# Rows of q, X and the output ordered by parity, and the filter turned by parity, in a gated mix of an FFT convolution and an MLP

## The chip, the cores and the metric

The kernel runs on one core of a Trainium2 chip. Its engines each work through their own queue in order: TensorE (PE in the profile; PEld is its weight loads), VectorE (DVE), ScalarE (ACT), GpSimd (POOL) and the sync engine (SP), which here issues DMAs. Matmuls write to PSUM; VectorE and ScalarE bring the results back to SBUF. The metric is the device time of one execution in microseconds (us). Before the change it is 241.14 us, the median of three runs (241.05 to 241.84).

## The reference

Three things are computed from `x = q` (2048 rows of 640) and mixed by a gate per row.

```python
g = sigmoid((q * gate_w).sum(-1, keepdims=True))
# A: a long convolution along the rows, one filter per column
kv = k_shift * v                       # k_shift: 4 taps of k along the rows
y  = irfft(rfft(pad(kv)) * rfft(pad(ssm_k)))[:2048] + kv * ssm_D
a  = q * y
# B: a mixer and an MLP
h  = gelu(layernorm(q) @ w1)           # its four column groups are then shifted
x1 = q + shifted(h) @ w2               # by 1, -1, 2, -2 rows
b  = x1 + gelu(layernorm(x1) @ w3) @ w4
out = g * a + (1 - g) * b
```

Inputs and output are bf16.

## The kernel before

**Layout.** The 2048 rows are 128 groups of 16. A group lies on one partition (`q_rows`, `o_rows`, `v_rows`, `k_rows`: partition p holds rows 16p to 16p + 15), and the 16 places in a group are called t1. X, the output and the q tiles have group p on partition p. V, and k by way of its transposes, are ordered by parity instead: partitions 0 to 63 hold the even groups and 64 to 127 the odd ones (`HALF`). V gets that order from an indirect DMA that GpSimd issues with a list of row numbers (`take`, `v_load`, `row_order`).

**The convolution** is a Fourier transform of 4096 points in steps. `tap` makes kv: four taps of the turned k by matmuls on four 32-row array tiles, and products with V. `step1` transforms over the partitions, for kv (`KV`) and for the filter (`HT0`). For kv the two parities are two matmuls, each with 64 contraction rows, on the upper and the lower half of the array (line 424); for the filter they are two matmuls with all 128 rows, against a table `F1N` made for the plain order (line 422). The filter comes in with channels on partitions and is turned by 16 transposes of 128x128 for each of five column blocks (`h_transpose`, line 395). Results go to DRAM scratch (`S_x`, `S_h`) and come back in another order (`gather`); `step2` transforms over the 16 places; `product` multiplies; `step3` goes back, by way of scratch `S_g` and `gin`; `step4` is the last inverse step: two matmuls of 128x320 that add up in one PSUM bank, against two tables in `F4` with zeros in every second column (line 882), then times the gate and q, and added to the MLP's result in X.

**The MLP.** `x_stats`, `x_norm` and `x_turn` normalise and turn four chunks of four places; `mlp1` multiplies by w1; `h_shift` builds the shifted rows, with `turn` for those that pass to the neighbour group (one copy by one partition-row of columns); `w2`, `x1_norm`, `w3`, `w4` follow. `store` writes two places (or one) at a time.

**Order.** Everything is issued in an order written out by hand as a list of steps (`ORDER`), a name, its arguments, the engine for each eviction (A or V) and a part. Each engine takes its instructions in that order. PSUM has 4 banks for the convolution (`psc`) and 2 pairs for the MLP (`psm`). The places in the shared SBUF rings are written out as well (`SLOTS`); the ring "row" has four places, for k, normalised chunks, step 1 and step 3 results, q tiles and the last gin tile. DMAs from hardware queues share eight completion semaphores in turn, so that an issue also waits for the landing of the eighth issue before it.

The lines that matter below: 422 and 424 (step 1), 395 (transposes of the filter), 369 and 371 (evictions on ScalarE and VectorE), 587, 596, 599, 602 (taps: matmuls, copies, products), 707 (mlp1), 784 (w2), 832 (w3), 854 (w4), 882 to 896 (step 4), 174 (indirect DMA), 190 and 193 (X loads), 215 (w4 load), 534 (gin), 846 (stores), 865 (q loads).

Of the kernel before, what the change touches and what calls it, by code (L numbers as in the profile page):

```python
# [16 lines left out]
P = 128  # L17
# [4 lines left out]
H = 64  # L22
# [19 lines left out]
def kernel(  # L42
# [24 lines left out]
        "c": "012312031203132103210322130123013021203123012032112300312012013021302101320130213102301230132103"  # L67
             "120132013023102302101301231201032013210312031203021321002312032012332013210132032101203103212033"
             "021320121031302210321301302310212032031210323101032210323103201302131022310132031202130213021302"
             "130310231032301230120",  # L70
        "m": "0101011010101010101010101010101010101010101010101010101010100101010",
        "row": "01230120312013312013021032103213201202020",
        "gt": "012301212210202103201301201",
        "xt": "010101",
        "gq": "01221011201201201210201210201201201",
        "ax": "0123230123102301",
        "hp": "01231203",
# [31 lines left out]
    F1N = const.tile([P, 2, H, 2], BF16, name="F1N")  # L109
    F4 = const.tile([P, 2, H, 2], BF16, name="F4")  # L110
# [65 lines left out]
    def flat(x):  # L176
        return x.rearrange("p t d -> p (t d)")
# [10 lines left out]

    def load_x(c):
        SP.dma_start(out=flat(X[:, 4 * c:4 * c + 4, :]), in_=q_rows[:, 4 * c * D:4 * c * D + 4 * D])  # L190

    def load_x0(h):
        SP.dma_start(out=flat(X[:, 2 * h:2 * h + 2, :]), in_=q_rows[:, 2 * h * D:2 * h * D + 2 * D])
# [92 lines left out]
    def f1n_table():  # L286

        ts(col(27), bit(0), -1.0, pf[:], op1=ALU.add)
        ts(col(28), col(27), 0.5)
        n = tab([P, H, 2], "n")  # L290
        ts(n[:, :, 0], R64[:, 0:H], col(27), col(28))
        ts(n[:, :, 1], n[:, :, 0], float(128 + 128), op0=ALU.add)
        ts(n[:, :, 0], n[:, :, 0], float(64 + 128), op0=ALU.add)
        yield from sin_table(F1N[:, 0], n, 256)
        yield
        V.tensor_scalar(out=F1N[:, 1], in0=F1N[:, 0], scalar1=bit(0), scalar2=None, op0=ALU.mult)
        V.tensor_tensor(out=F1N[:, 0], in0=F1N[:, 0], in1=F1N[:, 1], op=ALU.subtract)

    def f4_table():
# [11 lines left out]
        V.memset(F4[:], 0.0)  # L311
        yield from sin_table(F4[:, 0, :, 0], n, 256)
        A.activation(out=F4[:, 1, :, 1], in_=n[:], func=ACT.Sin, scale=TWO_PI / 256 * SH, bias=NPI[:])
# [70 lines left out]
    def h_transpose(dc, ev):  # L384
        if "HT0" not in st:
            st["HT0"] = main.tile([P, NT * D], BF16, name="HT0", tag="RT")
        hv = st.pop(("HN", dc)).rearrange("p (q t1) -> p t1 q", t1=NT)
        dst = st["HT0"][:].rearrange("p (t d) -> p t d", t=NT)
        def make(hh):
            box = {}  # L390

            def first():
                ps = box["ps"] = slot(psc, [P, 8, P], BF16, "pst", "c", 4)
                for i in range(8):
                    PE.transpose(out=ps[:, i, :], in_=hv[:, 8 * hh + i, :], identity=IDB[:])  # L395

            def second():
                evac(ev[hh], dst[:, 8 * hh:8 * hh + 8, dc * P:(dc + 1) * P], box["ps"][:])
            return first, second

        return banks(2, make)
# [7 lines left out]
    def step1(name, c, ev):  # L409
# [5 lines left out]
        def make(u):  # L415
            ps = []

            def first():
                for r in range(2):
                    ps.append(slot(psc, [P, 512], F32, "ps1", "c", 4))  # L420
                    if name == "HT0":
                        PE.matmul(ps[r][:], lhsT=F1N[:, r].rearrange("p a b -> p (a b)"), rhs=src[:, o + 512 * u:o + 512 * u + 512], start=True, stop=True)  # L422
                    else:
# [686 lines left out]
```

## Time and profile before

| | |
|---|---|
| median of three runs | 241.14 us |
| profiled execution: its time, its span | 242.25 us, 240.5 us |
| TensorE busy, share of the span | 223.2 us, 93% |
| VectorE busy | 188.6 us, 78% |
| ScalarE busy | 178.4 us, 74% |
| GpSimd busy | 16.4 us, 7% |
| granted TensorE clock, mean | 0.993 |
| DMA: moved, mean rate | 57.10 MB, 237 GB/s |
| matmuls of filter step 1 (L422) | 40, mean 379 ns |
| matmuls of kv step 1 (L424) | 40, mean 382 ns |
| transposes of the filter (L395) | 80, mean 226 to 228 ns |
| matmuls of step 4 (L882) | 64, mean 299 ns |

The profile is of one execution, in microseconds from the start of its span. An instruction's duration includes the passage through the pipeline, so that matmuls overlap and a mean of 380 ns stands beside a start every 216 ns; times of whole blocks in the chain of waits are the better price. The chain follows the work that ended last back from its end. A table of waits gives, for an engine and line, what it waited for, the total, the times, and the longest. Stretches give busy time of each engine, the granted clock and the DMA share.

### The profile page before, as it was taken

The numbers are of one execution on the slowest core, as the hardware profiler recorded it, in microseconds if no ns is written. First come the engines' busy times: TensorE is split into PE (matmuls) and PEld (weight loads), VectorE is DVE, ScalarE is ACT, GpSimd is POOL, SyncE is SP. The second block draws the span as 40 slices with busy tenths as digits, with TensorE's granted clock in tenths as the row PEclk, the third lists the DMA queues.
The fourth block names the chain that finished last, engine by engine and source line by source line (L and its number), as shares of the span: only waits on it lengthen the run. The fifth ranks groups of instructions, "written<-read, shape, count | busy, mean of one in ns | idle before, by whom it ended". The sixth has DMA issues, their size and how long they took to land.

```text
span 240.5 us, 5957 instructions
## 1 busy us (share of the span) xinstructions
PE 223.2 (93%) x2401; PEld 113.3 (47%) x2420; DVE 188.6 (78%) x448; ACT 178.4 (74%) x320; POOL 16.4 (7%) x34
## 2 busy tenths in 40 slices
PE   8669679999999999999799999999999999999993
PEld 3455345433656555444345344444444455447551
DVE  6899587989999999974658896395995997308994
ACT  4599957989978998899977698769777543447480
POOL 3172202000000020022200000000000000000000
PEclk9999979999999999999999999999999999999999
DMA  6999975460599799999795928099755113889664
GB/s 222 371 376 408 369 168 139 92 237 1 221 326 417 222 328 285 269 415 344 226 294 142 178 96 277 4 343 311 168 188 220 59 54 118 267 303 375 225 252 187
DMA packets 42889, 57.10 MB, mean 237 GB/s; under 512 B 20329, under 2 KB 35690, under 8 KB 42606
## 3 DMA queue, kind: packets, MB, share of 16 engines
q1 hardware_dynamic: 42286, 54.10, 68.8%
q0 software_dynamic: 576, 2.62, 2.7%
q8 instruction: 19, 0.31, 0.5%
q14 instruction: 8, 0.07, 0.1%
HBM read 34.42 MB, written 18.36 MB: 219 GB/s over the span
## 4 chain that ended last, share of the span: by engine, by line
PE 74%; DMA 17%; DVE 4%; SPq 2%; issue 1%; POOL 1%; ACT 0%; DVEq 0%
PE ps L854 19%; PE ps L832 19%; PE psw L784 9%; PE psm L707 7%; DMA W<-in_B_w_dram 5%; DMA KV<-in_A_v_dram,ROWS 5%; PE ps L462 4%; DMA X<-in_A_q_dram 4%; PE ps L422 4%; PE ps L509 3%; DMA gin<-S_g 3%; PE ps L424 3%; PE pst L395 2%; PE psk L587 2%; PE ps L882 2%; DVE b L682 1%
## 5 line engine op out<-in xcount | busy, mean ns | idle before, releaser
L854 PE MATMUL ps<-W,gt 128*128 128x128 bf16 (+1 forms) x370 | 55.0, 296 | 2.5 <-DMA W<-in_B_w_dram 1.2
L832 PE MATMUL ps<-x1t,W 128*128 128x512 bf16 x240 | 55.2, 380 | 0.2 <-ACT gt L837 0.2
L854 PEld LDWEIGHTS <-gt 128*128 128x128 bf16 x384 | 29.0, 98 | 26.6 <-issue 4.8
L832 PEld LDWEIGHTS <-W 128*128 128x128 bf16 x240 | 22.2, 98 | 28.2 <-issue 4.2
L837 ACT ACTIVATE gt<-ps 128x1024 bf16<-128x1024 f32 x24 | 24.8, 1034 | 7.6 <-PE ps L832 7.6
L369 ACT CAST stg<-ps 128x512 bf16<-128x512 f32 x47 | 25.5, 598 | 6.2 <-PE ps L424 4.0
L369 ACT CAST gs<-ps 128x320 bf16<-128x320 f32 x42 | 15.6, 434 | 16.2 <-PE ps L509 10.4
L707 PE MATMUL psm<-xt,WA 128*128 128x512 bf16 x100 | 25.0, 396 | 0.5 <-DVE xn L661 0.5
L371 DVE CAST stg<-ps 128x512 bf16<-128x512 f32 x33 | 21.9, 686 | 1.8 <-PE ps L424 0.8
L784 PE MATMUL psw<-WA,HT 128*128 128x512 bf16 (+1 forms) x111 | 20.8, 296 | 0.2
L369 ACT CAST hs<-ps 128x512 bf16<-128x512 f32 x28 | 15.0, 597 | 5.9 <-PE ps L462 5.9
L886 ACT ACTIVATE y<-ps,GS 128x320 bf16<-128x320 f32 x25 | 11.9, 526 | 7.2 <-PE ps L882 4.7
L371 DVE CAST gs<-ps 128x320 bf16<-128x320 f32 x22 | 10.1, 485 | 7.9 <-PE ps L509 6.5
L371 DVE CAST XS<-ps 128x512 bf16<-128x512 f32 x15 | 10.0, 686 | 7.4 <-PE ps L462 7.1
L707 PEld LDWEIGHTS <-WA 128*128 128x128 bf16 x100 | 9.3, 101 | 12.7 <-issue 3.5
L369 ACT CAST XS<-ps 128x512 bf16<-128x512 f32 x25 | 13.5, 595 | 2.1 <-PE ps L462 2.1
L784 PEld LDWEIGHTS <-HT 128*128 128x128 bf16 x116 | 10.0, 98 | 10.5 <-PE ps L424 0.7
L861 DVE SCALAR_TENSOR_TENSOR X<-ps,OMG,X 128x640 bf16<-128x640 f32 x15 | 13.2, 877 | 0.4 <-PE ps L854 0.3
L462 PE MATMUL ps<-ax,CMP 64*32 64x384 bf16 (+3 forms) x512 | 13.1, 300 | 0.0
L786 DVE SCALAR_TENSOR_TENSOR X<-psw,X 128x640 bf16<-128x640 f32 x16 | 12.9, 816 | 0.1
L789 ACT ACTIVATE jk<-X 128x640 bf16<-128x640 bf16 x16 | 12.3, 767 | 0.0
L487 DVE TENSOR_TENSOR XS<-XS,hs 128x2560 bf16<-128x2560 bf16 x8 | 11.9, 1485 | 0.1
(151 smaller groups left out, 342.8 us busy)
## 6 DMA issues: line engine op xcount, KB each, us to landing
S_x<-stg SPq DMA_DIRECT2D x8, 640.0 KB, 4.0
S_h<-stg SPq DMA_DIRECT2D x8, 640.0 KB, 8.6
ax<-S_x SPq DMA_DIRECT2D x8, 640.0 KB, 6.0
ax<-S_h SPq DMA_DIRECT2D x8, 640.0 KB, 5.6
S_g<-gs SPq DMA_DIRECT2D x8, 640.0 KB, 4.8
W<-in_B_w_dram SPq DMA_DIRECT2D x2, 1920.0 KB, 10.6
kn<-in_A_k_dram SPq DMA_DIRECT2D x4, 640.0 KB, 11.0
q<-in_A_q_dram SPq DMA_DIRECT2D x4, 640.0 KB, 5.0
```

The lines of the kernel that those rows point to most:

```text
L369: A.copy(out=dst, in_=src)
L371: V.tensor_copy(out=dst, in_=src)
L462: PE.matmul(ps[j][q:q + 32, lo - 512 * u:hi - 512 * u], lhsT=CMP[HALF[j], 8 * b + 4 * h + i, c, :], rhs=st[name, 2 * b + h][HALF[j], i, lo ...
L487: V.tensor_tensor(out=x, in0=x, in1=h, op=ALU.mult)
L707: PE.matmul(ps[:, v, :].rearrange("p (a b) -> p a b", a=4), lhsT=W1N[:, k, 160 * f:160 * f + P] if f < 4 else W1M[:, k, :], rhs=xt[:, :, k ...
L784: PE.matmul(ps[:, o:o + w], lhsT=h_tile(f, t1), rhs=W2P[:, f, o:o + w], start=(f == 0), stop=(f == 4))
L786: V.scalar_tensor_tensor(out=X1[:, t1, :], in0=ps[:], scalar=1.0, in1=X[:, t1, :], op0=ALU.mult, op1=ALU.add, accum_out=S12[:, 0, t1:t1 + 1])
L789: A.activation(out=jk[:], in_=X1[:, t1, :], func=ACT.Square, accum_out=S12[:, 1, t1:t1 + 1])
L832: PE.matmul(ps[:, u, :].rearrange("p (a b) -> p a b", a=4), lhsT=st["W3"][:, k, f * P:(f + 1) * P], rhs=xt[:, :, k, :], start=(k == 0), st ...
L837: A.activation(out=gt[:, 2 * (fp % 2):2 * (fp % 2) + 2, :], in_=ps[:], func=ACT.Gelu_apprx_tanh)
L854: PE.matmul(to[:, 0:w], lhsT=st["gt", c, f // 4][:, f % 4, i * P:(i + 1) * P], rhs=st["W4"][:, f, o:o + w], start=(f == 0), stop=(f == FC ...
L861: V.scalar_tensor_tensor(out=X1[:, t1, :], in0=ps[:], scalar=OMG[:, t1:t1 + 1], in1=X1[:, t1, :], op0=ALU.mult, op1=ALU.add)
```

## The change

X, q and the output take the order by parity that V and k had. So:

- The first X chunk comes as half loads of 64 partitions, even groups issued by the sync engine and odd groups by ScalarE (`load_half`); so does the second. The third and fourth X chunk and the four q tiles are gathered by GpSimd (`take`). `row_order` stands earlier.
- The filter is turned by parity: 64 transposes of 64x64 for each column block, on the four 64x64 tiles of the array, into two banks at once. Step 1 of the filter then uses the same table and the same two 64-row matmuls as kv; `F1N` and `f1n_table` go.
- Step 4's two matmuls go to the two column halves of the array and of the PSUM bank, with one table of 64 columns and no zeros; they no longer add up.
- `turn`, which moves rows to the neighbour group, needs two copies in place of one.
- Every store is two of 64 partitions; the second half of the very last is issued by ScalarE.
- `ORDER` and `SLOTS` are written anew throughout: w1, k, X and V loads, taps, mlp1 and the filter's parts change places; before the first product with V there are now the statistics of all four X chunks and 25 matmuls of mlp1 instead of 15; the w4 load stands ahead of three of the filter's sends to scratch.

```diff
-    F1N = const.tile([P, 2, H, 2], BF16, name="F1N")
-    F4 = const.tile([P, 2, H, 2], BF16, name="F4")
+    F4 = const.tile([P, H], BF16, name="F4")
...
+    def load_half(e, r, t, n):
+        e.dma_start(out=flat(X[HALF[r], t:t + n, :]), in_=q_rows[r:P:2, t * D:(t + n) * D])
+
     def load_x(c):
-        SP.dma_start(out=flat(X[:, 4 * c:4 * c + 4, :]), in_=q_rows[:, 4 * c * D:4 * c * D + 4 * D])
+        if c == 1:
+            load_half(SP, 0, 4, 4)
+            load_half(A, 1, 4, 4)
+        else:
+            take(flat(X[:, 4 * c:4 * c + 4, :]), q_rows, 4 * c)
...
-        SP.dma_start(out=flat(X[:, 2 * h:2 * h + 2, :]), in_=q_rows[:, 2 * h * D:2 * h * D + 2 * D])
+        load_half(SP, 0, 2 * h, 2)
+        load_half(A, 1, 2 * h, 2)
...
-        V.memset(F4[:], 0.0)
-        yield from sin_table(F4[:, 0, :, 0], n, 256)
-        A.activation(out=F4[:, 1, :, 1], in_=n[:], func=ACT.Sin, scale=TWO_PI / 256 * SH, bias=NPI[:])
+        yield from sin_table(F4[:], n, 256)
...
+            for t1 in range(NT):
+                for g in range(2):
+                    for r in range(2):
+                        PE.transpose(out=ps[g][HALF[r], t1, :], in_=hv[HALF[g], t1, r:P:2], identity=IDB[HALF[g], H * g:H * g + H],
+                                     tile_position=(H * g, H * r))
+        def second(g):
+            evac(ev[g], dst[:, :, dc * P + H * g:dc * P + H * g + H], ps[g][:])
...
-                    if name == "HT0":
-                        PE.matmul(ps[r][:], lhsT=F1N[:, r].rearrange("p a b -> p (a b)"), rhs=src[:, o + 512 * u:o + 512 * u + 512], start=True, stop=True)
-                    else:
-                        PE.matmul(ps[r][:], lhsT=F1[HALF[r]].rearrange("p a b -> p (a b)"), rhs=src[HALF[r], o + 512 * u:o + 512 * u + 512], start=True, stop=True,
-                                  tile_position=(H * r, 0))
+                    PE.matmul(ps[r][:], lhsT=F1[HALF[r]].rearrange("p a b -> p (a b)"), rhs=src[HALF[r], o + 512 * u:o + 512 * u + 512], start=True, stop=True,
+                              tile_position=(H * r, 0))
...
-            E.tensor_copy(out=dst[:, :, 1:P], in_=src[:, :, 0:P - 1])
+            E.tensor_copy(out=dst[:, :, 1:H], in_=src[:, :, H:P - 1])
+            E.tensor_copy(out=dst[:, :, H:P], in_=src[:, :, 0:H])
...
-        SP.dma_start(out=o_rows[:, a * D:(a + n) * D], in_=flat(X1[:, a:a + n, :]))
+        for r in range(2):
+            (A if r and a == LAST else SP).dma_start(out=o_rows[r:P:2, a * D:(a + n) * D], in_=flat(X1[HALF[r], a:a + n, :]))
...
-        SP.dma_start(out=flat(q2[:]), in_=q_rows[:, 4 * c * D:4 * c * D + 4 * D])
+        take(flat(q2[:]), q_rows, 4 * c)
...
-                    PE.matmul(ps[:], lhsT=F4[:, r].rearrange("p a b -> p (a b)"), rhs=g[:, r, o + 320 * v:o + 320 * v + 320], start=(r == 0), stop=(r == 1))
+                    PE.matmul(ps[HALF[r]], lhsT=F4[:], rhs=g[:, r, o + 320 * v:o + 320 * v + 320], start=True, stop=True, tile_position=(0, H * r))
```

## The prediction

> **What bounds the kernel now.** I read the chain of waits first, then the busy times of chosen stretches, then the instructions around single blocks, then the table of waits. Columns of the chain: start us, duration us, what.
>
> ```profile
> 19.06 11.65 DMA KV<-in_A_v_dram,ROWS
> 30.82 0.70 DVE KV L602
> 31.57 1.36 PE psk L587 x64
> 32.93 3.60 PE psm L707 x10
> ...
> 45.63 0.37 PE ps L424 x2
> ...
> 64.23 3.01 PE pst L395 x48
> ...
> 68.59 0.54 PE ps L424 x4
> 69.13 1.46 PE psw L784 x10
> ...
> 76.43 0.86 PE ps L422 x4
> 77.29 1.36 PE psw L784 x10
> ...
> 103.15 12.46 DMA W<-in_B_w_dram
> ...
> 217.30 7.33 DMA gin<-S_g
> ```
>
> Four regimes. Until 30.8 the start waits for the last V rows. From 45.6 to 103 the chain is TensorE without a gap. At 103 the w4 load stands in it. From 116 to 214 it is TensorE again. After that comes a tail.
>
> ```profile
> core 0: us, PE busy (x) PEld busy (x) DVE busy (x) ACT busy (x) POOL busy (x), PEclk, DMA share, GB/s
> 30.80:45.60 14.80, 13.94 (x338) 7.77 (x337) 13.12 (x35) 10.79 (x20) 1.21 (x2) 0.88 0.46 113
> 45.60:60.00 14.40, 14.12 (x86) 4.83 (x86) 12.95 (x39) 12.51 (x22) 0.00 (x0) 1.00 0.47 137
> 72.00:100.00 28.00, 27.84 (x197) 15.57 (x199) 27.23 (x68) 25.34 (x55) 1.21 (x2) 1.00 0.97 308
> 228.00:234.00 6.00, 5.95 (x43) 3.59 (x42) 6.00 (x20) 4.70 (x11) 0.00 (x0) 1.00 0.58 224
> ```
>
> To be seen: in the middle TensorE is full, but VectorE (27.23 of 28.00) is nearly so, and in the tail VectorE is full too. A shorter matmul helps only until the next engine is full.
>
> ```profile
> 36.69 0.26 PE L587 MATMUL psk<-DG,KW 32*128 32x32 bf16 x12
> 36.79 0.76 PE L587 MATMUL psk<-DG,KT 32*128 32x128 bf16 x48
> ...
> DVE KV L602 <- DMA KV<-in_A_v_dram,ROWS: 3.5, 1, 3.5
> DVE q L892 <- PE ps L882: 10.4, 2, 10.0
> ```
>
> The first two rows (timeline) price short matmuls on array tiles: 12 of them leave in 0.10 us, 8.3 ns each. The other two (waits: total us, times, longest) say that VectorE stands 3.5 us for V at the start and 10 us for the first inverse step in the tail.
>
> **The change part by part.** The profiled execution has a span of 240.5 and a time of 242.25 us, 1.1 above the median 241.14 of the three runs. The sum is of differences, so I take it from the median.
>
> *Filter step 1 (20 pairs of 128x512 matmuls).* A pair with 128 rows costs 0.43 (0.86 for 4). The V side already has the form that the filter gets: 4 in 0.54, and the block behind it takes 1.46 in place of 1.36, so a group of 4 costs 0.64. The pairs come as 10 groups of 4: 6.4 in place of 20 x 0.43 = 8.6. TensorE: -2.2.
>
> *Turning the filter.* Now 80 transposes in 3.01 + 2.15 = 5.16 us. The new 320 of 64x64 go round four array tiles. At the 8.3 ns of the taps they take 2.7, with three changes of tile form at 0.2 and one V-side group split by them (0.1) 3.4: -1.8. At the mean of a whole tap block (76 in 1.02, 13.4 ns) it is 5.0: -0.2. Upper end: weight loads of different tiles do not overlap, and each column costs what it costs now (3.01 us / 48 / 128 = 0.49 ns); 320 x 64 columns take 10.0, with the changes 10.7: +5.5. I take -1.7, by the taps, whose matmuls are the shortest on tiles in the trace.
>
> *What of these -3.9 reaches the end.* VectorE gets 8 more turn copies (the halved rows; about 0.18 each, as the 128x127 copies of 0.18 to 0.20), +1.4, loses two filter-table products (0.25 + 0.23), one normalisation (0.44) and three evictions (33 to 30, 0.69 each) to ScalarE, which gains 1.8 + 0.9. Over 45.6 to 100, VectorE's 51.3 becomes about 49.8, ScalarE's 47.9 about 50.6, TensorE's 53.9 about 50.0. Three engines within 2% cannot all run full; with the fullest at 96 to 97% the stretch takes 52.5 in place of 54.4. I take -1.9, ends 0 and -3.9.
>
> *Start.* The GpSimd queue issues X, V, X, V, V, then an rstd pair, then the last V: two 640 KB X transfers stand ahead of V. V's first packet in the trace's DMA records moves 4.6 us after its issue (13.2 to 17.9). Row order is computed earlier now and the first chunk's rstd is released about when it is now, so the first X issue is at 11.7 and data flow from 16.4. The sync queue's 4.7 MB (X halves, k, w1) are through by 15 at the 0.35 to 0.40 MB/us that the stretches before 27 move; its next item, a DMA transpose, waits for normalised X and holds back the filter and w2 loads. So six transfers, 3.9 MB, have the engines alone: 0.40 MB/us (2.62 MB in 2.7% of 16 engines' span) gives 26.2, plus 1 to landing, against 30.8; behind the second rstd (about 20.5 plus the 1.0 us issue, 4.6, 1.6 of data, 1 to landing) 28. At the rate V had beside other loads (2.62 MB from 19 to 30.8, 0.22) it is 35.2.
> VectorE then is the gate. Before V it loses the inverse-filter table (five rows, 1.3) and a memset (0.2), gains two rows of statistics (2.2), one large and two small k evictions less one x eviction (0.8), a shift copy (0.3), less a normalisation (0.4): 21.9 busy between 3.9 and 30.8 becomes 23.3. It idles about 2 us more before k lands (8.8), since the tables no longer fill that time. First V product: 3.9 + 23.3 + 2.3 = 29.5. From there TensorE's order holds 25 matmuls of mlp1 where it held 35, but two taps stand side by side, the second waiting 1.3 for its banks: 0.7 + 1.4 + 2.9 (the ten, between the 3.60 and 2.27 of the chain) + 1.1 + 1.3 + 1.1 + 1.2 + 1.1 + 2.3 = 13.1, so step 1 starts at 42.6, or at 43.3 if the last tap's eviction (0.7) shows, against 45.6. I take -2.3; ends +3.4 (V at 35.2) and -3.9 (V at 28 gating, VectorE never late). The three issues on ScalarE (0.43 each) lie before its first activation or between two; cover gone, +0.9.
>
> *w4 load.* In the sync order it now precedes three filter sends instead of following all of them. Today it leaves 5.8 us after the last w2 matmul (97.35), and TensorE idles 1.2. -0.8; ends 0 and -1.2.
>
> *Tail.* Step 4's 64 matmuls (8.7 us) become 32 pairs at once: 4.4 plus some 8 changes of form at 0.2, -2.7 on TensorE, but VectorE has the same 48 products and sums and is full. Cover gone, it would be worth at most 2.7. The four q loads leave the sync queue, where one held a gin load up to 217.30 and one, waiting 5.3 us for a q tile, held the last; that frees the 0.4 to 0.8 idle at 224.7. On GpSimd they wait with nothing behind them. The last is first used some 24 VectorE instructions (about 10 us) after its slot is free and needs 4.6 + 1.6 + 1 = 7.2: hidden; else up to +2. Nine more sync-queue stores at 0.40 are 3.6 us over the last ten; the final one is split, its half on ScalarE behind nothing. I take -0.5; ends +1 and -1.5.
>
> Sum: -2.3 - 1.9 - 0.8 - 0.5 = -5.5, that is **235.6 us**.
>
> **A rule against it.** The four V issues on GpSimd took 0.94 to 1.16 us although VectorE was busy 9.8 of 10.1 us beside some of them; my sum uses 1.0. The Trainium skill, SBUF — State Buffer, section "SBUF: two separate sides", says that a DMA issued from GpSimd is starved of descriptors while VectorE runs in a mode that takes the shared port, and names 620 ns growing to 3100 ns; its advice would be against gathering q there. By that figure six issues at about 3.1 in place of 1.0 would put V some 12 us later and the end near 247. This trace, with 1.16 as its longest issue, does not show it; it has 0.02 of the chance.
>
> **The rivals.**
> 1. *The middle gains nothing.* VectorE and ScalarE take over at once. For: 27.23 of 28.00. Against: ScalarE has 2.7 us of room in that stretch. -1.9 and half of the w4 gain fall away: 238.0.
> 2. *Slower: V comes late.* The six GpSimd transfers move at 0.22 MB/us: first product at 35.2, start +3.4, and TensorE, idle longer, runs its ten matmuls at the 3.60 of today, +0.7 on my 2.9: 241.1 + 3.4 + 0.7 - 3.2 = 242.0. It decides once V lands after about 34. For: landings of 9.9 to 12.8 us in the trace. Against: those shared the engines with sync loads that now come later.
> 3. *No faster: the 64x64 weight loads queue.* +5.5 in place of -1.7, and TensorE alone bounds: middle -2.2 + 5.5 = +3.3, total 240.8. For: the 32x64 weight load of L509 lasts 101 ns, not less than a 128x128 one (98). Against: sixteen such matmuls finish in 0.41 us. The Trainium skill, TensorEngine Tiling (Array Packing), section "Restrictions and Gotchas", names column tiling as excluding fast weight load, which would point this way; no row here shows such loads as the limit.
> 4. *Better all round.* Every lower end at once but the tail's: -3.9 - 3.9 - 1.2 - 0.5 = -9.5: 231.6.
>
> **How the numbers follow.** Forecast 0.42 (own range 234 to 237.5), rival 1 0.19, rival 2 0.15, rival 3 0.10, rival 4 0.11, the port 0.02, the rest 0.01. A change of 0.3% (0.7 us) is about what a measurement here can tell. Faster: 0.42 + 0.19 + 0.11 and a little of 2 and 3, 0.75. Within: 0.06. Slower: 0.19. The range runs from rival 4 to just beyond rival 2: 231 to 243.
>
> **What would show it.** First V product (KV after the 3.5 us wait) at 29 to 30, and that wait gone; step 1 of V from 43; filter step 1 as groups of 4 in 0.54; a block of 64 transposes in about 0.6 us (2 us means rival 3); VectorE and ScalarE above 95% between 45 and 100; no TensorE wait at the first w4 matmul; VectorE still full in the tail. Wrong if V lands after 34, if ScalarE's queue delays the first statistics, or if the doubled stores reach past the last sum.

## The result and the profile after

The change made the kernel slower: 255.23 us (median of 4 runs, 254.18 to 257.31) against 241.09 beside it, a ratio of 1.059 (95% interval 1.051 to 1.067). The forecast was 235.6, the range 231 to 243. The profiled execution, the slowest of the four, took 257.31 us with a span of 255.0, which is 14.5 more than the span of before.

The chain of waits of the changed kernel; columns start us, duration us, what:

```profile
10.41 19.44 DMA kn<-in_A_k_dram
29.90 2.33 PE pst L606 x20
...
57.03 0.54 PE ps L414 x4
...
78.18 3.64 PE pst L389 x100
...
87.66 3.67 PE pst L389 x128
...
92.79 0.54 PE ps L414 x4
93.33 1.47 PE psw L776 x10
...
132.65 9.16 DMA ax<-S_h
```

The late V rows are gone from the chain. In their place stands the last k load, issued at 10.4 and landed at 29.9. The first product with V comes at 40.2 in place of 30.8, although V's last packet is in at 30.6. Step 1 of V (L414) starts at 57.0, where it started at 45.6. The filter is turned (L389) in blocks of 64 that take 1.8 us and more; the prediction had 0.6. The wait for w4 at 103 is gone, and one for the filter's first gathers stands at 132.

The table of waits, us in total, times, longest, first of the changed kernel:

```profile
DVE q L885 <- PE ps L875: 10.3, 1, 10.3
PEld L606 <- DMA kn<-in_A_k_dram: 8.3, 4, 4.8
DVE b L672 <- DMA X<-in_A_q_dram: 6.4, 3, 3.6
ACT jk L666 <- DMA X<-in_A_q_dram: 4.3, 1, 4.3
PE ps L452 <- DMA ax<-S_h: 1.6, 2, 1.2
```

and of the kernel before:

```profile
PEld L616 <- DMA kn<-in_A_k_dram: 4.0, 3, 2.6
DVE b L682 <- DMA X<-in_A_q_dram: 1.2, 2, 0.6
ACT jk L676 <- DMA X<-in_A_q_dram: 0.9, 1, 0.9
```

VectorE no longer waits for V. TensorE's weight loads wait twice as long for k, and VectorE and ScalarE wait 10.7 us for X where they waited 2.1. ScalarE issues its half load of the second chunk only behind the activation that waits for the first chunk, so that this load leaves at 9.07 us. In the tail VectorE waits for the first inverse step about as long as before (10.3 against 10.0).

The busy times of chosen stretches, first of the kernel before, then of the changed one:

```profile
core 0: us, PE busy (x) PEld busy (x) DVE busy (x) ACT busy (x) POOL busy (x), PEclk, DMA share, GB/s
10.00:17.00 7.00, 5.27 (x69) 4.08 (x68) 6.19 (x23) 6.94 (x11) 4.45 (x7) 1.00 1.05 384
17.00:25.00 8.00, 6.85 (x96) 4.39 (x97) 7.87 (x23) 7.88 (x14) 2.40 (x3) 1.00 1.02 408
```

```profile
10.00:17.00 7.00, 5.45 (x53) 4.85 (x51) 4.13 (x20) 5.12 (x7) 5.07 (x6) 0.58 1.10 236
17.00:25.00 8.00, 5.91 (x29) 2.94 (x28) 6.21 (x22) 5.75 (x7) 3.09 (x5) 0.72 1.01 393
25.00:31.00 6.00, 1.73 (x14) 1.21 (x13) 1.78 (x5) 0.61 (x2) 0.36 (x1) 0.77 0.65 243
...
57.00:72.00 15.00, 14.50 (x85) 4.95 (x86) 11.98 (x43) 13.01 (x23) 0.00 (x0) 1.00 0.46 159
72.00:111.00 39.00, 38.69 (x523) 22.91 (x527) 32.80 (x77) 31.47 (x56) 1.42 (x3) 1.00 0.82 269
232.00:251.00 19.00, 17.36 (x144) 9.33 (x142) 18.95 (x53) 11.78 (x25) 0.94 (x1) 1.00 0.84 254
```

From 10 to 17 us the DMA engines are as busy as before (last column but one) and move 236 in place of 384 GB/s. From 25 to 31 the engines that compute stand idle for most of the time. From 72 to 111 TensorE is full and VectorE is not (32.80 of 39.00). In the tail VectorE is full, as before.

The same by five marks, each the start of the first instruction of its kind in the two traces, or the end of the span:

```
                               before    after    difference   gained or lost since the mark above
first product with V             30.8     40.2        +9.4         +9.4
step 1 of V starts               45.6     57.0       +11.4         +2.0
first w3 matmul                  97.6    111.3       +13.7         +2.3
last block of 40 w3 matmuls     205.4    220.0       +14.5         +0.8
end of the span                 240.5    255.0       +14.5          0.0
```

So the loss is made before 57 us, between 57 and 111, and a little (0.8) behind that. The page's row of the granted TensorE clock shows a companion of the first part (40 slices of the span, tenths of full speed; the changed kernel, then the kernel before):

```profile
PEclk9857779869999999999999999999999999999998
PEclk9999979999999999999999999999999999999999
```

TensorE idles in the late start, and the clock falls to half in four spells (11.2 to 18.0, 21.4 to 24.8, 28.2 to 35.1, 48.7 to 55.5 us in the trace), where the kernel before has one (32.2 to 35.6): the last ten mlp1 matmuls ahead of step 1 take 3.06 in place of 2.26 us. The Trainium skill, TensorE: Matmul & The Clock Gate, section "What's actually happening", says that the clock is halved after an idle window of about 3.4 us and counted in such windows; the spells here last 6.83 or 3.41 us, which agrees in length.

### The profile page after: what moved, and what is told of

It reads as the page before. It is cut to its first block, busy times and chain, and to the rows that moved or that the text cites. A ratio compares the mean times of both kernels' runs of the same rounds, so it can differ in the third digit from the quotient of the medians.

```text
span 255.0 us, 6462 instructions
## 1 busy us (share of the span) xinstructions
PE 232.0 (91%) x2639; PEld 116.9 (46%) x2660; DVE 193.9 (76%) x460; ACT 172.3 (68%) x306; POOL 22.5 (9%) x40
## 4 chain that ended last, share of the span: by engine, by line
PE 67%; DMA 16%; DVE 10%; ACT 2%; issue 2%; POOL 0%; SPq 0%; ACTq 0%
PE ps L824 21%; PE ps L847 14%; DMA kn<-in_A_k_dram 10%; PE psw L776 9%; PE psm L697 4%; PE ps L452 4%; PE ps L414 4%; PE pst L389 4%; DMA ax<-S_h 4%; PE ps L499 3%; DVE X L889 2%; DVE q L882 2%; DMA S_x<-stg 2%; PE psk L577 2%; PE pst L606 1%
## 5 line engine op out<-in xcount | busy, mean ns | idle before, releaser
L697 PE MATMUL psm<-xt,WA 128*128 128x512 bf16 x100 | 27.5, 427 | 2.6 <-DVE WA L209 2.1
L361 ACT CAST gs<-ps 128x320 bf16<-128x320 f32 x38 | 14.2, 433 | 16.3 <-PE ps L499 8.6
L363 DVE CAST stg<-ps 128x512 bf16<-128x512 f32 x30 | 19.7, 686 | 5.3 <-PE ps L414 4.6
L361 ACT CAST hs<-ps 128x512 bf16<-128x512 f32 x25 | 13.6, 594 | 7.6 <-PE ps L452 7.6
L363 DVE CAST XS<-ps 128x512 bf16<-128x512 f32 x20 | 13.2, 685 | 5.5 <-PE ps L452 5.5
L363 DVE CAST gs<-ps 128x320 bf16<-128x320 f32 x26 | 11.6, 485 | 5.9 <-PE ps L499 4.3
L452 PE MATMUL ps<-ax,CMP 64*32 64x128 bf16 (+3 forms) x512 | 13.4, 300 | 1.6 <-DMA ax<-S_h 1.6
L606 PE MATMUL pst<-IDB,kn 128*128 128x128 bf16 x80 | 8.3, 277 | 6.9 <-DMA kn<-in_A_k_dram 6.9
L672 DVE BATCH_NORM_STATS2 b<-X 128x6 f32<-128x320 bf16 x22 | 9.5, 474 | 6.4 <-DMA X<-in_A_q_dram 6.4
L361 ACT CAST XS<-ps 128x512 bf16<-128x512 f32 x20 | 11.1, 589 | 3.6 <-PE ps L452 3.6
## 6 DMA issues: line engine op xcount, KB each, us to landing
kn<-in_A_k_dram SPq DMA_DIRECT2D x4, 640.0 KB, 10.7
```

Of the source, the lines that this page charges most:

```text
L361: A.copy(out=dst, in_=src)
L363: V.tensor_copy(out=dst, in_=src)
L452: PE.matmul(ps[j][q:q + 32, lo - 512 * u:hi - 512 * u], lhsT=CMP[HALF[j], 8 * b + 4 * h + i, c, :], rhs=st[name, 2 * b + h][HALF[j], i, lo ...
L606: PE.transpose(out=ps[:, i - a, :], in_=src()[:, i * P:i * P + P], identity=IDB[:].rearrange("p (q r) -> p r q", r=2) if by_parity else ID ...
L697: PE.matmul(ps[:, v, :].rearrange("p (a b) -> p a b", a=4), lhsT=W1N[:, k, 160 * f:160 * f + P] if f < 4 else W1M[:, k, :], rhs=xt[:, :, k ...
```

## The experiments

Two theories of the late start were put against each other. A: tiny packets. The load of the shift taps (`cr`, 640 packets of 8 bytes) stands between w1 and the last k load in the sync queue and lets a k packet through only after many gathered ones. B: rate. The half loads of X move too slowly, wherever `cr` stands.

**Taps ahead of w1** (e1_cr_first)

```diff
-        "load_x.3:0 k_load.0.AAV:1 x_norm.0.VVAV:0 load_w1:0 x_norm.0.VVAV:1 k_load.2.VAV:6 v_load.3:0 load_cj:0 "
+        "load_x.3:0 k_load.0.AAV:1 x_norm.0.VVAV:0 load_cj:0 load_w1:0 x_norm.0.VVAV:1 k_load.2.VAV:6 v_load.3:0 "
```

> The changed kernel with one line of the order moved: the load of the shift taps (cr, 640 packets of 8 bytes) is issued ahead of the w1 load instead of behind it, so that it no longer stands between w1 and the last k load in the sync queue. Theory A (tiny packets): from 18.7 us on, one 8-byte packet of cr passes for each gathered 5120-byte packet of 0.2 us, and the last k load waits behind them; it landed at 29.9 us. With cr ahead it lands by about 20 to 21, the first V product comes at about 31 to 32 instead of 40.2, step 1 of V at about 46 to 47 instead of 57.0, and the time falls by about 10 to about 245 us. Theory B (rate): the half loads and the gathered traffic move too few bytes, wherever cr stands; the last k load still lands after 27 and the time stays within 2 us of 255.

**Taps in 128 packets** (e2_cr_128)

```diff
-        SP.dma_start(out=st["cr"][:], in_=A_shift_k.rearrange("(k p) j -> p k j", p=P))
+        SP.dma_start(out=st["cr"][:], in_=A_shift_k.rearrange("(p k) j -> p k j", p=P))
```

> The changed kernel with the shift taps loaded in 128 packets of 40 bytes instead of 640 of 8, in the same place of the queue and with the same bytes. (The taps then belong to other channels: the output differs by that alone.) Theory A (each packet of cr costs one turn of a gathered packet, 0.2 us; 40 packets an engine become 8): the wait of the last k load shrinks from about 8 to about 1.6 us, it lands at about 22 to 24, time about 246 to 249 us. Theory B (rate, bytes): nothing changes, 255.

Measured: 251.30 us with the taps ahead (1.040, 1.034 to 1.046) and 249.32 with 128 packets (1.033, 1.025 to 1.040), 4 to 6 us off the 14. Theory A had asked for 245 from the first and 246 to 249 from the second. In the trace's packet records the last k packet starts at 23.1 and 22.8 us, against 29.0 in the changed kernel. So A is real: fewer packets of the same bytes let k through 6 us earlier. But step 1 of V starts at 50.6 and 48.6, not at 46 to 47. The chain of the run with 128 packets shows why:

```profile
8.59 9.25 DMA X<-in_A_q_dram
17.86 0.90 DVE b L672 x2
...
20.23 5.10 PE psm L697 x15
25.33 0.24 PE pst L606 x4
...
48.65 0.54 PE ps L414 x4
```

The half load that ScalarE issues lands at 17.9; VectorE's statistics wait for it, w1's regrouping stands behind them, fifteen mlp1 matmuls wait for that and run mostly at half clock (20.6 to 24.0; 5.10 us), and the turning of k stands behind those on TensorE.

**Half loads cut by columns** (e4_x_columns)

```diff
-        e.dma_start(out=flat(X[HALF[r], t:t + n, :]), in_=q_rows[r:P:2, t * D:(t + n) * D])
+        t, n = t + r * (n // 2), n // 2
+        e.dma_start(out=flat(X[:, t:t + n, :]), in_=q_rows[:, t * D:(t + n) * D])
```

> The changed kernel with the six half loads of X cut by columns instead of by partitions: each still moves the same bytes on the same queue at the same place, but to all 128 partitions. (The first two chunks of X then hold rows in another order: the output differs by that alone.) The half loads' packets of 5120 bytes took 300 to 560 ns against 200 for other loads. If packets to 64 partitions are slow for their place (theory B), those packets fall to the rate of 41 to 51 ns a KB, the stretch from 10 to 17 us moves about 0.35 in place of 0.24 MB a us and everything behind it lands 2 to 3 us earlier: time about 252 to 253, and by theory B in full (the rate holds up the last k load) about 247. Theory A: the last k load still stands behind cr's packets, gains at most those 2 to 3 us, time 252 to 255.

Measured: 246.15 us, 1.018 (1.012 to 1.024). The gain is 9 us, the full amount of theory B. One other thing changes with the cut: the statistics of a place can start when one of the two loads is in; the run to every second partition below leaves that as it was. Stretches of this run:

```profile
10.00:17.00 7.00, 4.64 (x51) 3.33 (x50) 6.76 (x22) 6.77 (x10) 5.53 (x7) 1.00 1.06 378
25.00:31.00 6.00, 4.68 (x154) 2.88 (x157) 5.79 (x25) 5.66 (x13) 1.24 (x2) 1.00 0.02 6
```

The rate is back at 378 GB/s and all loads are through by 26. The taps' packets are in by 13.6 us, ahead of the first gathered packet (14.4): where the halves are quick, the tiny packets cost nothing. In the changed kernel 480 of the 640 are through by 16.8, and only the other 160, still queued when the gathered packets begin at 18.1, need until 27.2. Theory A acts only where B has made the queue late. ScalarE's half of the second chunk also leaves earlier here, at 5.69 in place of 9.07.

**Half loads of neighbouring rows** (e5_half_dest) and **to every second partition** (e14_every_second), in place of the same line:

```diff
-        e.dma_start(out=flat(X[HALF[r], t:t + n, :]), in_=q_rows[r:P:2, t * D:(t + n) * D])
+        e.dma_start(out=flat(X[HALF[r], t:t + n, :]), in_=q_rows[HALF[r], t * D:(t + n) * D])   # e5
+        e.dma_start(out=flat(X[r:P:2, t:t + n, :]), in_=q_rows[r:P:2, t * D:(t + n) * D])      # e14
```

> The changed kernel with its six half loads kept on 64 partitions each, but every half reads 64 neighbouring rows of q instead of every second one (the first two chunks of X then hold rows in another order, which alone changes the output). It tells the two things apart that the cut by columns changed at once. If the 64 partitions are what makes the packets slow (place theory), the half loads' 5120-byte packets keep their 300 to 560 ns, the last k load lands at 27 to 30 us and the time is about 255. If reading every second row is what makes them slow (source theory), the packets fall to about 200 ns, the last k load lands before 20 and the time is about 246 to 247, as with the cut by columns.

> The changed kernel with its six half loads still of 64 partitions and 64 packets each, from the same rows of q, but written to every second partition of all 128 instead of to one half of them (the first two chunks of X then hold rows in another order, which alone changes the output). If the number of partitions or of packets makes them slow, their 5120-byte packets keep about 340 ns, the first tap stays at about 36 us and the time at about 255. If it is that all 64 lie in one half of the memory, the packets fall to about 200 ns, the last k load is through by 16, the first tap comes at about 25 and the time is about 246. The Trainium skill, SBUF — State Buffer, section Door 1: The DMA port swizzle, says the second: partitions 0 to 63 reach 8 of 16 ports, and its formula gives every second partition all 16.

Measured: 254.86 us with neighbouring rows (1.055, 1.050 to 1.060), 248.16 to every second partition (1.028, 1.019 to 1.037). The stretch from 10 to 17 us, first e5, then e14:

```profile
10.00:17.00 7.00, 3.87 (x64) 3.40 (x62) 4.38 (x21) 5.18 (x7) 4.72 (x6) 1.00 1.07 217
```

```profile
10.00:17.00 7.00, 6.00 (x72) 5.59 (x70) 6.60 (x29) 5.39 (x7) 4.90 (x6) 0.76 1.05 386
```

The packet records of the traces, mean duration in ns:

```
                                        before  after   e4    e5   e14
ScalarE's half of chunk 1, 5120 bytes      -     340     -    384   196   (64 packets)
w1, 1280 bytes, 640 packets               57      93    58    101    56
V and X gathered, 5120 bytes             203     208   201    211   201
last k packet starts, us                   -    29.0  15.1   28.7  17.9
```

The source rows are not it (e5: 384 ns). For ScalarE's load of the second chunk it is not the number of partitions or packets either (e14: 64 of each, 196 ns). It is that all 64 partitions lie in one half (here 64 to 127); and w1's packets, which go to all 128, are slowed beside them (93 and 101 against 57). The Trainium skill, SBUF — State Buffer, section "Door 1: The DMA port swizzle", says that partitions 0 to 63 reach 8 of 16 ports and 64 to 127 the other 8, at half the rate; its formula gives every second partition all 16. The trace agrees: 340 against 196 ns. e14 keeps 7 of e4's 9 us. It is 2 us above e4 although its packets are quick from 9 us on: from 4 to 6 us, around the half loads of the first chunk, it moved 0.32 MB (the changed kernel 0.47, e4 0.82), its k packets took 425 ns on average (e4 211), and its first tap comes at 28.2 and not at 24.9. So for the first chunk the place in memory is not the whole cause; the rest stays open.

**The second chunk gathered by GpSimd** (e10_c1_gather)

```diff
     def load_x(c):
-        if c == 1:
-            load_half(SP, 0, 4, 4)
-            load_half(A, 1, 4, 4)
-        else:
-            take(flat(X[:, 4 * c:4 * c + 4, :]), q_rows, 4 * c)
+        take(flat(X[:, 4 * c:4 * c + 4, :]), q_rows, 4 * c)
```

> The changed kernel as it stands, but the second chunk of X is gathered by GpSimd like the third and fourth, and issued at about 3.5 us, in place of the two 320 KB half loads on the sync queue and on ScalarE; the first chunk keeps its half loads. If the half loads of that chunk (64 packets of 300 to 560 ns each, the second half not issued before 9 us) are what holds up the start, w1 and the last k load come through by about 16, the first tap moves from 36.9 to about 25 to 27 and the time falls from 255 to 246 to 248 us, near the cut by columns (246.15). If the four small half loads of the first chunk matter as much, it stays above 250.

Measured: 250.10 us, 1.038 (1.033 to 1.044), less of a gain than expected. The bytes come through (376 GB/s from 10 to 17, last k packet at 17.5). Its chain shows what is late now:

```profile
2.61 8.47 DMA kn<-in_A_k_dram
11.13 2.19 PE pst L602 x20
...
14.73 0.81 DVE b L668 x2
...
20.29 5.08 PE psm L693 x15
```

The gather of the second chunk moves from 8.5 us, beside the early k loads: the one that TensorE works on lands at 11.1, VectorE reaches the second chunk's statistics at 14.7 (12.9 in e4), and the fifteen mlp1 matmuls again run mostly at half clock (21.6 to 25.0), 5.08 us where e4 has 3.40. The first chunk's half loads are still there; whether they or the gather make that k load late was not separated.

Then the middle. **The filter turned in 160 tiles of 128x64** (e3_turn_tall), on the changed kernel:

```diff
...
             for t1 in range(NT):
-                for g in range(2):
-                    for r in range(2):
-                        PE.transpose(out=ps[g][HALF[r], t1, :], in_=hv[HALF[g], t1, r:P:2], identity=IDB[HALF[g], H * g:H * g + H],
-                                     tile_position=(H * g, H * r))
+                for r in range(2):
+                    PE.transpose(out=ps[t1 // 8][HALF[r], t1 % 8, :], in_=hv[:, t1, r:P:2], identity=IDB[:], tile_position=(0, H * r))
...
```

> The changed kernel with the filter turned by 160 transposes of 128 rows by 64 columns (column tiles alone) in place of 320 of 64 by 64. In the trace the 320 took 9.2 us, 28.6 ns each. If a transpose costs by its columns whatever its rows and neighbours (rival 3 of the prediction: nothing overlaps), 160 take 4.6 us: TensorE 4.6 us shorter between 74 and 92, the time 2.5 to 4.6 lower, 251 to 253 us. If four array tiles do overlap and it is the records alone that look long, two tiles overlap half as well and nothing is won: 255, or more.

Measured: 255.79 us (1.055, 1.046 to 1.064), no change. Both readings offered were wrong in part. In the records of the instructions' starts a round of four 64x64 transposes takes about 112 ns and a round of two 128x64 ones about 110: the members of a round do start together, a few ns apart, and the round costs the same with half as many members.

**The filter turned on row tiles alone** (e15_turn_rows), with the half loads cut by columns:

```diff
             for t1 in range(NT):
                 for g in range(2):
-                    for r in range(2):
-                        PE.transpose(out=ps[g][HALF[r], t1, :], in_=hv[HALF[g], t1, r:P:2], identity=IDB[HALF[g], H * g:H * g + H],
-                                     tile_position=(H * g, H * r))
+                    PE.transpose(out=ps[g][:, t1, :], in_=hv[HALF[g], t1, :], identity=IDB[HALF[g], H * g:H * g + H],
+                                 tile_position=(H * g, 0))
```

> The changed kernel with the half loads cut by columns (246.15 us) and the filter turned by 160 transposes of 64 rows by 128 columns on two row tiles, the columns of the array undivided (the filter's rows then stand in natural order, which alone changes the output further). If any division of the array makes a round cost about 110 ns, 80 rounds take 8.8 us and the time stays at about 246. If it is the division by columns (two tiles that share their rows load one after the other, and slowly), a round of two row tiles costs about 62 ns, 80 rounds take 5.0 us, and the time falls by 3 to 4, to about 242 to 243, as with the filter's part undone. The Trainium skill, TensorE: Matmul & The Clock Gate, section The mechanism, says that weight loads overlap only where the rows differ, and its section on loading the stationary operand prices a load by its columns, whatever the rows; the page TensorEngine Tiling (Array Packing) adds that column tiling has no fast weight load. By these the second.

Measured: 244.56 us, 1.013 (1.004 to 1.021), beside 1.018 for e4: less than the 242 to 243 expected, and the intervals overlap. The blocks themselves are plain. One block of each form from the timelines, e3 first, then e15:

```profile
78.78 3.78 PE L388 MATMUL pst<-IDB,E 128*64 128x128 bf16 x64
```

```profile
67.00 2.19 PE L389 MATMUL pst<-IDB,E 64*128 64x64 bf16 x64
```

A round of two row tiles takes 62 ns, like a whole transpose in the kernel before. So the division by columns costs it. From the start of step 1 of V to the first w3 matmul this run needs 52.9 us, e4 55.8; the transposes alone are 3.9 shorter. Its profiled run also starts step 1 of V 1.7 later; what takes the rest of the gain stays open. The Trainium skill, TensorE: Matmul & The Clock Gate, section "The mechanism", says that weight loads overlap with running matmuls only where the rows differ: by that, two column tiles that share their rows load in turn, which fits 110 against 62. The Trainium skill, TensorEngine Tiling (Array Packing), section "Restrictions and Gotchas", adds that column tiles have no fast weight load; no run here separates the two.

**The whole filter part undone** (e7_filter_back), with the half loads cut by columns:

```diff
...
-                for g in range(2):
-                    for r in range(2):
-                        PE.transpose(out=ps[g][HALF[r], t1, :], ...
+                PE.transpose(out=ps[t1 // 8][:, t1 % 8, :], in_=hv[:, t1, :], identity=IDB[:])
...
+                    if name == "HT0":
+                        PE.matmul(ps[r][:], lhsT=F1N[:, r].rearrange("p a b -> p (a b)"), rhs=src[:, o + 512 * u:o + 512 * u + 512], start=True, stop=True)
+                    else:
...
```

> The changed kernel with the half loads cut by columns (246.15 us) and the filter's part of the change undone: 80 transposes of 128x128, the two 128-row tables, 20 pairs of 128-row matmuls in the filter's first step, and the three small table instructions put back on VectorE and ScalarE. By the traces the turning took 9.2 us as 320 tiles (a round of four takes 112 ns) against 5.0 whole (62 ns each), and the pairs 0.32 in place of 0.43: undoing gives 4.2 back and costs 2.2, so TensorE gains 2.0 between 60 and 101. Theory C (the filter part is a loss): 243.5 to 245, the first w3 matmul about 2 us earlier than 100.8. Theory D (the loss of the middle comes from the new order of the instructions, not from the transposes): 246 to 247, no change, the time saved is idle elsewhere.

Measured: 242.08 us, 1.002 (0.999 to 1.005): 4 us better than e4, and level with the kernel before. By its matmuls the filter part should cost 2.0 (9.2 against 5.0 us of transposes, less 2.2 of pairs). The intervals of the two ratios leave 2 to 6 for the difference. The traces show what the rest can be. In e4 TensorE is full with a block of 64x64 transposes from 66.1 to 69.7, and the granted clock is halved right behind it:

```profile
66.06:69.70 3.64, 3.64 (x130) 3.60 (x130) 1.95 (x5) 2.62 (x3) 0.20 (x1) 1.00 0.99 364
69.71:73.12 3.41, 3.19 (x13) 1.25 (x14) 2.43 (x5) 1.06 (x2) 0.00 (x0) 0.50 0.84 265
```

The ten w2 matmuls and the group of step 1 behind this block take 3.6 us, those behind the next block 2.0. A spell of 3.41 us begins within 0.8 us of the end of a block of 128 in six of the nine traces with these 64x64 transposes (e1, e4, e5, e8, e9, e14), and in none of the seven traces that turn the filter in another way. With such a spell the filter part would cost 3.6. No run tests the spell alone, so that this part of the cause is argued, not shown.

**Second chunk gathered, filter part undone** (e11_gather_filter), e10 and e7's edit together, and then **filter loads, w2 and gate weights ahead of the first DMA transpose** (e12_loads_up):

```diff
-        "tap.4.AVAV:0 ... x_norm.3.AVVV:3 x_turn.3.D:0 "
+        "tap.4.AVAV:0 ... x_norm.3.AVVV:3 load_h.0:0 load_h.1:0 load_w2:0 load_gw:0 x_turn.3.D:0 "
...
```

> As the run with the second chunk gathered by GpSimd, and the filter's part of the change undone as well. The filter part was worth 4.1 us on top of the cut by columns; the two add up if they lie in different stretches: 242 to 244 us, level with the kernel before or up to 1% above it. If they share a cover, less than 2 us of the 4.1 show.

> As the run before, and the first two filter loads, w2 and the gate weights issued in the sync queue ahead of the first DMA transpose, which waits for normalised X until about 30 us, instead of behind it. In the kernel as changed the DMA engines stand idle from 30 to 45 us and are full from 45 to 57, and the stores of step 1 land late (ScalarE waits 5.3 us for one, TensorE 0.3 to 1). If that wait and the later ones for stores and gathers come from the loads pushed into that stretch, the time falls by 1 to 3, to 239.5 to 242. If the stores land no earlier, no change.

Measured: 246.90 us (1.025, 1.019 to 1.030) and 248.10 (1.030, 1.025 to 1.036). The filter part is worth 3.2 here (1 to 5 by the intervals). Loading earlier gains nothing, although the loads leave at 11.4 to 14.0 in place of 39.3 us and later; the store that ScalarE waits for stands where it stood, in the chain of e12:

```profile
54.59 5.21 DMA S_x<-stg
```

The 5.2 us are the store's way from issue to landing; ScalarE's wait for it is 0.9 us in the first of the two runs and 0.7 in the second. So that wait is not due to the loads pushed into the stretch.

**The w4 load put back** (e8_w4_back), with the half loads cut by columns; in the order, the load moves from before the last filter evictions' sends to behind them, and the last two sends move ahead of the first w4 matmuls:

```diff
-        "... step1.HT0.0.VVVVVVAAVV:4 load_w4:0 swap.L1.L2.left:0 ... step2.x.3.AAVVVVVAAV:11 w4.1:0 "
-        "... step1.HT0.0.VVVVVVAAVV:16 step1.HT0.0.VVVVVVAAVV:15 "
+        "... step1.HT0.0.VVVVVVAAVV:4 swap.L1.L2.left:0 ... step2.x.3.AAVVVVVAAV:11 step1.HT0.0.VVVVVVAAVV:16 "
+        "step1.HT0.0.VVVVVVAAVV:15 load_w4:0 w4.1:0 "
```

> The changed kernel with the half loads cut by columns (246.15 us) and the w4 load put back behind the last filter sends in the sync queue, as it stood before. If the w4 load's new place is what makes the filter's first gathers late (TensorE waits 1.6 us or more for ax at 130 to 131, the DMA engines are full from 123 to 138), the gathers land earlier, that wait goes, and a wait for w4 of 1 to 2 us comes back at the first w4 matmul: the time within 1 us of 246.2. If the place of the load was a gain of its own (prediction: 0.8), the time rises by 0.8 or more, to about 247.

**The w4 load ahead, in the kernel before** (e13_before_w4), this part of the change alone:

```diff
-        "step1.HT0.0.AAVVAVVVAV:10 step1.HT0.0.AAVVAVVVAV:11 step1.HT0.1.AAAVAVVAAV:15 w3.0.2:1 "
+        "step1.HT0.0.AAVVAVVVAV:10 step1.HT0.0.AAVVAVVVAV:11 load_w4:0 step1.HT0.1.AAAVAVVAAV:15 w3.0.2:1 "
...
-        "step2.x.0.VVVAAAVAAV:3 load_w4:0 x1_norm.2.VAAV:1 "
+        "step2.x.0.VVVAAAVAAV:3 x1_norm.2.VAAV:1 "
```

> The kernel before with one part of the change alone: the w4 load issued ahead of three filter sends in the sync queue, at about 97.5 instead of 103.2 us. The prediction priced this at 0.8, at most 1.2, the wait of TensorE at the first w4 matmul: 240.1 to 240.9 against 241.3. On top of the cut by columns, putting the load back cost 2.9 us. If the load's place is worth that here too, 238.5; if the sends and the gathers behind it pay for it, 241 or more.

Measured: 249.00 us with the load put back (1.032, 1.028 to 1.037; e4 has 1.018), and 240.33 for the kernel before with the load ahead against 241.27 (0.997, 0.993 to 1.002). In the waits of e8, and of e4:

```profile
PE ps L848 <- DMA W<-in_B_w_dram: 2.5, 1, 2.5
```

```profile
PE ps L453 <- DMA ax<-S_h: 1.7, 2, 1.2
```

The two waits change places, as expected, but not at par: behind the sends the load costs 2.9 us in the new order (3.5 by the ratios, 1.6 to 5.4). In e8 the clock is halved from 119.6 to 123.0 behind the wait, and the first ten w4 matmuls after it take 3.85 us in place of e4's 2.32. The load leaves at 110.0, 10.1 us after the first w3 matmul; in the kernel before it leaves 5.5 after it, and TensorE waits 1.2. In the old order it is worth about the 0.8 of the prediction, not clear of noise. This is the only version whose median comes out below the kernel before.

**Step 4 as before** (e9_step4_back), with the half loads cut by columns:

```diff
...
-                    PE.matmul(ps[HALF[r]], lhsT=F4[:], rhs=g[:, r, ...], start=True, stop=True, tile_position=(0, H * r))
+                    PE.matmul(ps[:], lhsT=F4[:, r].rearrange("p a b -> p (a b)"), rhs=g[:, r, ...], start=(r == 0), stop=(r == 1))
```

> The changed kernel with the half loads cut by columns (246.15 us) and the last inverse step done as before, 64 matmuls of 128 columns in accumulating pairs instead of 32 pairs on two column tiles. The prediction: 2.7 us of TensorE, hidden behind a full VectorE, so the time stays within 0.7 us of 246.2. If VectorE's tail was waiting for TensorE, the time rises by up to 2.7, to about 249.

Measured: 246.62 us, 1.022 (1.017 to 1.026), 0.5 from e4 and inside its interval: hidden.

## Why the prediction was wrong

**Start, forecast -2.3, measured +11.4.** The step that failed is "The sync queue's 4.7 MB (X halves, k, w1) are through by 15 at the 0.35 to 0.40 MB/us that the stretches before 27 move". I took a rate measured on transfers to 128 partitions for transfers to 64. From 10 to 17 us 1.65 MB moved (0.24 MB/us), w1 came through at 18.7, and the last k load, which I had nowhere on the path, at 29.9. With the halves cut by columns the queue is through by 15.3, as the sentence says. The rest of the queue working held: the gathered data flow at 0.40 MB/us, and no issue on GpSimd took over 1.16 us. With the halves cut by columns the first V product stands at 29.45 us, against 29.5 forecast, which fits VectorE as the gate. From there to step 1 it took 15.5 us instead of 13.1 to 13.8 (step 1 at 45.0): TensorE waited four times, 0.5 to 1.2 us, among the taps, and its clock was halved from 39.0 to 42.4. Even then the start's gain is 0.6, not 2.3.

**Rival 2** had the sign and the stretch, but the wrong victim: V's last packet was in at 30.6, ahead of the 34 from which that rival decides, and its queue moved at full rate. Its price, +0.9 in all, came from V's landing alone; nothing in the prediction asked what stands behind a slow load in its own queue, or what the sync queue's small packets do once another queue is full.

**Middle, forecast -1.9, measured +2.3 in the trace, and 4 by the runs.** Filter step 1 came as priced: groups of 4 in 0.54 and blocks behind them at 1.46 to 1.47. The turning is the term that fell: "I take -1.7, by the taps, whose matmuls are the shortest on tiles in the trace". The taps are four row tiles with all 128 columns; the transposes divide the columns too. (The 0.2 for a change of tile form stands in no row; a w2 block behind a tiled group takes 1.46 in place of 1.36, 0.1 more.) The upper end, +5.5, was nearer: 9.2 us against 5.16, +4.0. So rival 3, at 0.10 of the chance, was near in its price, and right that weight loads on small tiles are not short (200 ns here for 64x64, 148 for whole ones). Its price was worked out from another reason, though: no overlap at all, and 0.49 ns for each column. By that a round of four 64x64 tiles would take 125 ns, of two column tiles 63 and of two row tiles 125; measured are 112, 110 and 62. Row tiles do overlap, and a column on a column tile costs nearly twice as much, so that the near price is partly luck. VectorE was not full in the middle (32.80 of 39.00), so that the co-bound, on which rival 1 rested, did not decide.

**w4 load, forecast -0.8.** Its size fits in the old order (-0.9, but with an interval of -1.6 to +0.4 not clear of nothing); in the new order its place is worth about 3, with the half clock behind the wait, while the filter's gathers, pushed back behind it, cost 1.6 at 132 us, a wait that the prediction did not name.

**Tail, forecast -0.5, measured 0.0.** Step 4's halves are hidden under VectorE, as said (0.5, within noise), the last q too. The last sum ends 0.9 earlier after the last w3 block, and the doubled stores give it back: 4.0 us from the last sum to the end of the span, 3.1 before.

**What is left.** Without half loads and without the filter part, 0.4 us (-0.3 to +1.3) remain above the kernel before, although the w4 load's gain is in. Against it stand waits for step 1's stores and for the filter's gathers, which the kernel before does not have in its chain. The store costs ScalarE 0.7 to 1.0 us. Whether the new order or the new places in the rings make them was not tried, beyond e12.

## What to carry to other kernels

A load's rate belongs to its destination as much as to its bytes: before splitting a transfer by partitions, ask whether each part spans the whole memory; here a cut by columns moved the same bytes at the full rate, and every second partition did so for the later loads. Price a matmul on array tiles by a row with the same division (rows or columns) and the same kind of weight load, not by the shortest tiled matmul to be found. And behind each slowed load, list what stands in the same queue: here the load that decided was the last k tile, two places behind.

## What the runs showed of the hardware

- ScalarE's load to the 64 partitions of the upper half took 340 to 404 ns for 5120 bytes a packet (the changed kernel, e1, e2, e5), against 196 to every second partition (e14) and 201 to 211 for gathers to 128; a load to all 128 that ran beside it slowed as well (1280 bytes: 91 to 101 against 56 to 58 ns).
- Beside a full gather queue, the 8-byte packets of the sync queue passed at 17 to 22 a microsecond, with 77 to 80 gathered packets of 5120 bytes (20 to 25 us): the last 160 of 640 needed from 18.1 to 27.2 us, while the first 480 had passed from 14.8 to 16.8, before the gathers began. In the kernel before, all 640 passed ahead of the gathers, from 14.4 to 17.0.
- A round of transposes with their data as weights takes 62 ns for a whole one, 62 for two on row tiles, about 110 for two on column tiles, about 112 for four on both. Dividing the columns makes a round cost nearly two whole transposes.
- In six of nine traces the granted clock was halved for 3.41 us from about the end of a block of 128 transposes of 64x64 (e4: 69.7 to 73.1), although TensorE was full in the window ahead of it (3.64 of 3.64 us).
